# Batch 1's last 256 tokens in 64-token chunks, its first state products and batch 0's half-row states as narrower matmul tiles

## The chip, the cores and the metric

The kernel runs on one core of a Trainium2 chip. The metric is the device time of one execution in microseconds (us). A core has TensorE for matmuls (PE in the profile, with PEld for its weight loads), VectorE (DVE), ScalarE (ACT), GpSimd (POOL), and SyncE (SP), which here issues the DMAs. Each engine works through its own queue of instructions in order and waits for the others by semaphores. Matmul results land in PSUM, eight banks of 128 partitions x 2 KB, from where DVE or ACT copy them to SBUF.

## The reference

Eight batches of 576 tokens, eight heads of 64. First a retention attention without softmax, then a feed-forward layer whose activation is a Silu with its own slope per column:

```
scores = scale * q @ k.T                       # per batch and head, 576 x 576
ret    = scores * gamma_h ** (i - j) for i >= j, else 0
x      = ret @ v                               # heads side by side: 4608 x 512
h      = x @ w_in                              # 512 -> 2048
out    = (h * sigmoid(beta * h)) @ w_out       # 2048 -> 512
```

As the decay is a product, `gamma ** i * gamma ** -j`, it is put into q and v as factors per token (`gq`, `gv`), and the attention can go chunk by chunk: in a chunk, masked scores times v; from all chunks before it, q times a state, which is the running sum of k.T @ v (64 x 64 per head).

## The kernel before

**Tiling.** Batches are worked on in the order 0 to 6, then a block of all batches' last 64 tokens, then 7. The first 512 tokens of a batch are one MLP block, and the eight last pieces of 64 tokens together make the ninth. For a block, `up` makes 128 columns of h for 512 tokens with four matmuls (over 128 rows of w_in each, `KO` = 4) and ACT's Silu writes `gT`; `down` makes 128 tokens of the output with 16 matmuls over `gT` and w_out. `up` can also do half of the tokens (256 columns). Its PSUM tiles come from the tag `mm`, which has three banks; the tags `O` and `sc` have two each, `st` one.

**Attention.** Heads go in four pairs; a pair fills 128 partitions, 64 per head. A state product over 128 tokens as a whole-row matmul computes 128 x 128 for a pair, of which the two 64 x 64 blocks on the diagonal are needed. `d_st`, `d_sc` and `d_out` (batches 2 to 7) work in chunks of 64 tokens with 64 x 64 tiles, four of which lie in different quarters of the PE array: states, scores, and outputs with what earlier chunks add (`cross`). `d_st` returns a `chain` that sums states on DVE into `warm` and `first` in turn and has ACT cast each sum to bf16 (`sbq`, halves of the `sbd` tiles). For heads 4 to 7 these batches hold k and q in another order of heads (`turned`, `head_of`). Batch 1 (`seq` indices 4 to 7) has its own functions with chunks of 128: `pre` and `pre_q` scale and cast, `t_q` and `t_k` transpose on PE, `a_sc` makes scores and masks them on DVE, `a_st` the states, which accumulate in PSUM, `a_O` the chunk's own output, `a_cross` what earlier chunks add with block-diagonal `sbds`, and `a_x` copies to `xT`. Batch 0 has functions `s_*` over two spans of 256 tokens. `s_st(a, n, s, rows)` makes the states of heads 4a to 4a + 3 and of span s over all 128 partitions or the lower or upper half of them; `s_keep` casts them into `sbds`.

**Order.** The schedule is written by hand, engine by engine as the calls come. The head is a straight list of calls (it starts with `warm_up`); in it `keep_warm` is a matmul of 512 columns whose result nobody reads. After it, the list `fill` holds the MLP's steps, and `streams` hold the rest, each with a place in `fill` before which it goes; `merged` weaves them. `d0` is where batch 0's `down` starts and `u1` where batch 1's `up` starts. Batch 1's first ten 128-column pieces of h are made in halves, all first halves and then all second ones, so that the second half of its attention (chunks 6 and 7) can go between them.

Of the kernel before, what the change touches and what calls it, by code (L numbers as in the profile page):

```python
# [11 lines left out]
F32 = mybir.dt.float32  # L12
# [7 lines left out]
def kernel(  # L20
# [46 lines left out]
    NQ = 6  # L67
    E = CB
    XB = 2
    QB = 2  # L70
    HT = MB // 2
    VB = 4
    q_tiles, kv_tiles = {}, {}
# [208 lines left out]
    def pre_q(b, n):  # L282

        if n == 0:
            batch[b] = dict(qs=sb.tile([P, CB, H, D], BF16, name="qs", tag="qs", bufs=2),
                            qT=sb.tile([P, CB, HP, P], BF16, name="qT", tag="qT", bufs=2))
        if b < 2:
            hs, cs = slice(n // 2 * HP, (n // 2 + 1) * HP), slice(n % 2 * 2, n % 2 * 2 + 2)
            e = nc.vector
        else:  # L290
            if n % 2:
                return
            cs = slice(n, n + 2)
            for to, hs in turned:
                nc.gpsimd.tensor_tensor(batch[b]["qs"][:, cs, to], q_tiles[b][:, hs, cs].rearrange("p h i d -> p i h d"),  # L295
                                        gq[:, cs, hs].unsqueeze(3).to_broadcast([P, 2, len(range(H)[hs]), D]), ALU.mult)
            return
        e.tensor_tensor(batch[b]["qs"][:, cs, hs], q_tiles[b][:, hs, cs].rearrange("p h i d -> p i h d"),
                        gq[:, cs, hs].unsqueeze(3).to_broadcast([P, cs.stop - cs.start, hs.stop - hs.start, D]),
                        ALU.mult)  # L300

    def pre(i, js=(0, 1)):

# [57 lines left out]
    def q_cols(i, r, p):  # L361

        b, c = seq[i]
        if b is None:
            return live[i]["qkT"][r, 0, p, :], lambda o: o
        return (batch[b]["qT"][r, :, p, c * PC:(c + 1) * PC], lambda o: o.rearrange("k (i s) -> k i s", i=CB))
# [31 lines left out]
    def a_cross(i):  # L398

        b, c = seq[i]  # L400
        if c == 0:
            return
        for p in range(HP):
            rhs, view = q_cols(i, slice(0, P), p)
            nc.tensor.matmul(view(O_of(i, p)), sbds[c - 1][:, p, :], rhs, start=False, stop=True, skip_group_check=True)

    def a_O(i):

        b, c = seq[i]
        L = live[i]  # L410
        new_O(i)
        R, vn = L["R"], L["vn"]
        for j, p in [(n % 2, n // 2) for n in range(H)]:
            nc.tensor.matmul(O_of(i, p)[j * D:(j + 1) * D], vn[:, 2 * p + j, :], R[:, j, p, :],
                             start=opens(i, p), stop=c == 0, skip_group_check=True)

    def a_x(i):
# [9 lines left out]
    def a_st(i):  # L427

        b, c = seq[i]
        if b is None:  # L430
            return
        L = live[i]
        if c == 0:
            state_ps[b] = psum.tile([P, HP, P], F32, name="st", tag="st", bufs=1)
        st = state_ps[b]
        for p in range(HP):
            nc.tensor.matmul(st[:, p, :], heads(L["kn"], p), heads(L["vn"], p),
                             start=(c == 0 and p == 0), stop=True, skip_group_check=True)
        for j in range(2):
            r, cols = slice(j * D, (j + 1) * D), slice(j * D, (j + 1) * D)  # L440
            e = nc.vector.tensor_copy if i in (CB + 2, CB + 3) else nc.scalar.copy
            if c < CB - 1:
                e(sbds[c][r, :, cols], st[r, :, cols])
                continue
            e(ends[b][r, :2], st[r, :2, cols])
            e(ends[b][(1 - j) * D:(2 - j) * D, 2:], st[r, 2:, cols])

    spread = [(0, 0), (1, 1), (0, 1), (1, 0)]

# [69 lines left out]
    def s_st(a, n, s, rows, at=None, fresh=False):  # L519

        if n not in s_sts:
            s_sts[n] = psum.tile([P, HP, P], F32, name="st", tag="mm" if n else "st", bufs=3 if n else 1)
            fresh = True
        S, at = spans[s], 2 * a if at is None else at
        for i in range(2):
            for p in range(2):
                nc.tensor.matmul(s_sts[n][:, at + p, :], heads(S["kn"][rows, i], 2 * a + p), heads(S["vn"][rows, i], 2 * a + p),  # L527
                                 start=fresh and i == 0 and p == 0, stop=True, skip_group_check=True)
# [25 lines left out]
    def after(later, earlier):  # L554
        tc.add_manual_dep(later.ins, earlier.ins.name, mybir.DependencyInfo(mybir.DependencyClass.Sync, mybir.DependencyReason.DATA))

    def d_sc(u):

        R = [sb.tile([P, 2, 2, HP, TL], BF16, name="R", tag="R", bufs=4) for _ in range(2)]
        sc = {}  # L560
        for x in range(2):
            for j in range(2):
                sc[x, j] = psum.tile([P, 2, HP, TL], F32, name="sc", tag="O" if x else "sc", bufs=2)
            for cl in range(2):
                for p in range(HP):
                    for j, hh in spread:
                        c = 4 * x + 2 * cl + hh
                        nc.tensor.matmul(columns(u, sc[x, j][half(hh), cl, p, :]), piece(u, c)["kT"][half(j), p, half(hh)],  # L568
                                         q_of(u, c, j, p), start=cl == 0 and p == 0, stop=True, skip_group_check=True)
        mask = tri[1 if u == B else 0][:].unsqueeze(1).to_broadcast([P, 2 * HP, TL])  # L570
        batch.setdefault(u, {})["R"] = R

        def masks(x):
            for j in range(2):
                nc.vector.tensor_tensor(R[x][:, j].rearrange("k c p q -> k (c p) q"),  # L575
                                        sc[x, j].rearrange("k c p q -> k (c p) q"), mask, ALU.mult)
        return masks

    def d_st(u, x):

        S = [psum.tile([P, 2, HP, D], F32, name="st", tag=t, bufs=n) for t, n in (("st", 1), ("mm", 3))]
        for cl in range(2):
            for p in range(HP):
                for hh, j in spread:
                    L = piece(u, 4 * x + 2 * cl + hh)
                    nc.tensor.matmul(S[hh][half(j), cl, p, :], L["kn"][half(hh), 2 * p + j, :],  # L586
                                     L["vn"][half(hh), head_of(u, p, j), :], start=cl == 0 and p == 0, stop=True,
                                     skip_group_check=True)

        def chain():  # L590
            for c in range(4 * x, 4 * x + 4):
                new, add = sums[c % 2], S[c % 2][:, c // 2 % 2]
                if c:
                    nc.vector.tensor_tensor(new[:], add, sums[(c - 1) % 2][:], ALU.add)  # L594
                else:
                    nc.vector.tensor_copy(new[:], add)
                nc.scalar.copy((sbq[c] if c < NC - 1 else ends[u])[:], new[:])  # L597
        return chain

    def d_out(u):  # L600
# [42 lines left out]
        return lambda: cross(1), evict  # L643


    gts = {}

    def up(m, fo, c0=0, cn=CB):
# [32 lines left out]
    def down(m, ms, f0, fn=4, n0=0, nn=d_model):  # L681
# [3 lines left out]
            pos_[ms] = psum.tile([P, d_model], F32, name="po", tag="mm" if m or ms < 3 else "st", bufs=3 if m or ms < 3 else 1)  # L685
        po = pos_[ms]
        for fo in range(f0, f0 + fn):
            parts = ((0, nn),) if m or fo < 5 else ((0, nn // 2), (nn // 2, nn))
            for x, y in parts:
                nc.tensor.matmul(po[:, x:y], gT[:, fo, ms, :], w_out_sb[:, fo, n0 + x:n0 + y],  # L690
                                 start=(fo == 0), stop=(fo == FO - 1), skip_group_check=m == 0)
        if f0 + fn < FO:
            return
        if m not in ots:
# [25 lines left out]
    def F(f, *a):  # L720
        return lambda: f(*a)
# [9 lines left out]
    t_q(0, 0)  # L731
    pre_q(0, 2)
    pre_q(0, 3)
    keep_warm()
    t_q(0, 1)
    keep_warm()
    pre_s(0, 0, 0)
    s_T(0, 0)
    pre_s(1, 0, 0)
# [7 lines left out]
    s_sc(1, 0, "mm")  # L747
    pre_s(0, 1, 0)
    pre_s(1, 1, 0)
    keep_warm("st")  # L750
    s_T(1, 1)
    s_sc(0, 1, "sc")
    pre_s(0, 1, 1)
    pre_s(1, 1, 1)
    s_st(0, 1, 0, whole_span)
    s_keep(0, 1, (act, act))
    s_st(0, 0, 0, low)
    s_keep(0, 0, (act, act))
    s_O(0, 0, "O")
    s_sc(1, 1, "mm")  # L760
    s_st(0, 1, 1, low)
# [48 lines left out]
    fill += [F(down_rows, n) for n in range(3)]  # L810
    fill += [F(down, 0, 3, 0)] + [F(down, 0, ms, f0) for f0 in (4, 8) for ms in range(4)] + [F(down, 0, ms, 12) for ms in (3, 0, 1, 2)]

    u1 = len(fill)
    fill += [F(up, 1, fo, 2 * x, 2) for x in range(2) for fo in range(10)]
    fill += [F(up, 1, fo) for fo in range(10, FO)]
    fill += [F(down, 1, ms, f0) for ms in range(MB // P) for f0 in range(0, FO, 4)]
    base = {1: u1 + 10}
    for n, m in enumerate(blocks[2:], 2):
        base[n] = len(fill)
        fill += [F(up, m, fo) for fo in range(FO)]  # L820
# [2 lines left out]
    fill += [F(down, blocks[-1], MB // P - 1, 0, FO, n0, nn) for n0, nn in ((0, 384), (384, 128))]  # L823

    def second(i):
        for f in (a_O, a_cross, a_x):
            f(i)
            f(i + 1)
        a_st(i + 1)

    def triangles():
        nc.gpsimd.memset(causal, 1.0)
# [2 lines left out]
        for t, pattern in zip(tri, ([[1, CB], [CB, TL // CB]], [[1, TL]])):  # L835
            nc.gpsimd.memset(t[:], 1.0)
            for x in range(2):
# [13 lines left out]
               [(d0 + 7, F(pre_q, 1, n)) for n in range(4)] + [(d0 + 12.5, F(pre_q, XB, n)) for n in range(4)] + [(d0 + 11.6, F(t_q, 1, 0)), (d0 + 12.6, F(t_q, 1, 1))],  # L851
               [(d0 + 8, F(pre, 4, (0,))), (d0 + 8, F(pre, 5, (0,))), (d0 + 9, F(pre, 4, (1,))), (d0 + 9, F(pre, 5, (1,))),
                (d0 + 12.7, F(t_k, 4)), (d0 + 14, F(t_k, 5)), (d0 + 14, F(a_sc, 4)), (d0 + 15, F(a_sc, 5)),
                (d0 + 15, F(a_st, 4)), (d0 + 15.9, F(second, 4))],
               [(d0 + 10, F(pre, 6, (0,))), (d0 + 10, F(pre, 7, (0,))), (d0 + 12, F(pre, 6, (1,))), (d0 + 12, F(pre, 7, (1,))),
                (d0 + 15.95, F(t_k, 6)), (u1 + 1, F(t_k, 7)), (u1 + 2, F(a_sc, 6)), (u1 + 3, F(a_sc, 7)),
                (u1 + 4, F(a_st, 6)), (u1 + 7, F(second, 6))]]


    def early_states(u):  # L860
# [85 lines left out]
```

## Time and profile before

| what | us |
|---|---|
| median of three runs | 297.1 (296.67 to 298.74) |
| the profiled execution | 297.28 |
| its span, first to last instruction | 295.5 |
| PE busy | 287.1 |
| ACT busy | 145.9 |
| POOL busy | 111.1 |
| DVE busy | 102.5 |

The profile is one execution. "Busy" is the time in which an engine has at least one instruction under way; matmuls are pipelined, so a matmul's own duration (about 0.2 to 0.4 us) is longer than the time until the next may start, and the time from start to start tells what a matmul costs in a row. The chain of work that ended last follows from the last instruction back to what released each step; its pieces in order of time show which engine set the pace where. "L690" is line 690 of the kernel: 690 is `down`, 655 `up`, 670 `ups` (`up` in two steps, for batch 0), 248 `keep_warm`, 352 `t_q`, 358 `t_k`, 474 and 475 `s_T`, 490 `s_sc`, 504 `s_O`, 512 `s_cross`, 527 `s_st`, 378 `a_sc`, 405 `a_cross`, 414 `a_O`, 437 `a_st`, 586 `d_st`, 568 `d_sc`, 614 and 627 `d_out`, 594 and 597 the sums and casts of `chain`.

### The profile page before, as it was taken

What the parts mean: (1) busy time and instruction counts of PE and PEld (TensorE: products, weight loads), DVE (VectorE), ACT (ScalarE), POOL (GpSimd) and SP (SyncE); (2) the same over time, 40 slices, a digit from 0 to 9 for tenths busy, and PEclk for the clock granted to TensorE, in tenths of its full rate; (3) what the DMA queues carried; (4) which work ended last, traced back from release to release, by engine and by line L of the source; (5) the groups of instructions that cost most, each with busy time, mean ns of one, the idle gap of its engine ahead of it and who ended that gap; (6) DMA issues with size and microseconds to landing.
All of it is one profiled execution on the core that took longest, in us unless ns stands there. A gap on an engine that the chain in (4) does not pass through costs nothing.

```text
span 295.5 us, 7656 instructions
## 1 busy us (share of the span) xinstructions
PE 287.1 (97%) x3245; PEld 150.6 (51%) x3274; DVE 102.5 (35%) x213; ACT 145.9 (49%) x255; POOL 111.1 (38%) x219
## 2 busy tenths in 40 slices
PE   7999999999999999999999999999999999999995
PEld 3654587855544554445444544454554544444443
DVE  5764546604640551045204530354053500110012
ACT  5657537783278434843474347434780167007600
POOL 5957027955733713280438316754223000000000
PEclk9999999999999999999999999999999999999999
DMA  7999999999999898949999849998998110131011
GB/s 225 306 367 386 376 226 277 220 180 253 222 229 235 214 162 231 252 72 161 231 250 198 180 105 273 190 177 180 219 174 138 73 38 0 35 71 38 0 71 71
DMA packets 124033, 53.97 MB, mean 183 GB/s; under 512 B 101840, under 2 KB 116448, under 8 KB 124000
## 3 DMA queue, kind: packets, MB, share of 16 engines
q1 hardware_dynamic: 123968, 53.49, 82.1%
q8 instruction: 25, 0.41, 0.6%
q14 instruction: 8, 0.07, 0.1%
q10 hardware_dynamic: 32, 0.01, 0.0%
HBM read 36.71 MB, written 9.44 MB: 156 GB/s over the span
## 4 chain that ended last, share of the span: by engine, by line
PE 96%; DMA 1%; issue 1%; ACT 0%; DVE 0%; DVEq 0%
PE po L690 42%; PE ph L655 38%; PE ph L670 4%; PE O L614 2%; PE sc L568 1%; PE st L586 1%; DMA qn<-in_q_dram 1%; PE O L627 1%; PE T L352 1%; PE st L527 1%; PE sc L378 0%; PE sc L490 0%; PE O L504 0%; ACT kT L475 0%; PE ph L248 0%
## 5 line engine op out<-in xcount | busy, mean ns | idle before, releaser
L690 PE MATMUL po<-w_out_sb,gT 128*128 128x512 bf16 (+3 forms) x619 | 125.7, 358 | 2.3 <-issue 2.1
L657 ACT ACTIVATE gT<-ph,beta_sb 128x512 bf16<-128x512 f32 (+1 forms) x140 | 91.5, 659 | 50.9 <-PE ph L655 50.5
L655 PE MATMUL ph<-xT,w_in_sb 128*128 128x512 bf16 (+1 forms) x550 | 114.4, 364 | 0.5
L690 PEld LDWEIGHTS <-gT 128*128 128x128 bf16 x636 | 60.2, 98 | 60.7
L655 PEld LDWEIGHTS <-w_in_sb 128*128 128x128 bf16 x560 | 54.3, 98 | 57.5 <-DVE first L594 0.4
L697 DVE COPY ot<-po 128x512 f32<-128x512 f32 (+2 forms) x33 | 22.2, 672 | 72.2 <-PE po L690 69.4
L328 POOL CAST kn<-kvn 128x128 bf16<-128x128 f32 (+2 forms) x76 | 23.4, 343 | 46.1 <-DMA kvn<-in_k_dram 41.2
L295 POOL TENSOR_TENSOR qs<-qn,gq 128x256 bf16<-128x256 f32 (+1 forms) x36 | 26.3, 756 | 33.1 <-DMA qn<-in_q_dram 33.1
L575 DVE TENSOR_TENSOR R<-sc,tri 128x512 bf16<-128x512 f32 x28 | 17.4, 684 | 60.0 <-PE sc L568 60.0
L306 POOL TENSOR_TENSOR vn<-kvn,gv 128x512 bf16<-128x512 f32 x28 | 29.1, 1040 | 7.4 <-DMA kvn<-in_v_dram 7.1
L642 ACT CAST xT<-O 128x512 bf16<-128x512 f32 x14 | 7.5, 590 | 31.6 <-PE O L627 31.6
L597 ACT CAST sbd<-warm 128x256 bf16<-128x256 f32 x18 | 7.3, 407 | 25.6 <-DVE warm L594 20.6
L670 PE MATMUL ph<-xT,w_in_sb 128*128 128x512 bf16 x54 | 12.8, 379 | 0.1
L594 DVE TENSOR_TENSOR first<-st,warm 128x256 f32<-128x256 f32 x24 | 10.2, 425 | 2.9 <-ACT sbq L597 0.5
L316 POOL TENSOR_TENSOR kn<-tln,gq 128x128 bf16<-128x128 f32 (+1 forms) x12 | 5.6, 470 | 14.2 <-DMA tln<-in_q_dram 9.9
L594 DVE TENSOR_TENSOR warm<-st,first 128x256 f32<-128x256 f32 x18 | 7.6, 423 | 9.6 <-PE st L586 8.4
L673 ACT ACTIVATE gT<-ph,beta_sb 128x512 bf16<-128x512 f32 x14 | 8.7, 688 | 4.4 <-PE ph L670 4.4
L642 DVE CAST xT<-O 128x512 bf16<-128x512 f32 x14 | 9.0, 686 | 5.1 <-PE O L627 5.1
L214 POOL CAST w_in_sb<-wt 128x256 bf16<-128x256 f32 (+1 forms) x15 | 7.7, 530 | 5.0 <-DMA wt<-in_moe_w_in_dram 4.9
L597 ACT CAST sbd<-first 128x256 bf16<-128x256 f32 x18 | 7.3, 407 | 2.2 <-DVE first L594 0.2
L670 PEld LDWEIGHTS <-w_in_sb 128*128 128x128 bf16 x56 | 5.2, 97 | 6.3 <-issue 0.5
L231 DVE TENSOR_SCALAR w_out_sb<-wt,rbeta_sb 128x512 bf16<-128x512 f32 x13 | 5.9, 485 | 5.0 <-DMA wt<-in_moe_w_out_dram 5.0
(107 smaller groups left out, 166.1 us busy)
## 6 DMA issues: line engine op xcount, KB each, us to landing
qn<-in_q_dram SPq DMA_DIRECT2D x16, 512.0 KB, 5.2
kvn<-in_k_dram SPq DMA_DIRECT2D x32, 256.0 KB, 6.1
kvn<-in_v_dram SPq DMA_DIRECT2D x32, 256.0 KB, 5.1
out_dram<-ot SPq DMA_DIRECT2D x31, 256.0 KB, 3.4
wt<-in_moe_w_out_dram SPq DMA_DIRECT2D x8, 512.0 KB, 8.5
wt<-in_moe_w_in_dram SPq DMA_DIRECT2D x5, 512.0 KB, 8.8
wt<-in_moe_w_in_dram SPq DMA_DIRECT2D x6, 256.0 KB, 5.6
tln<-in_q_dram SPq DMA_DIRECT2D x8, 128.0 KB, 3.6
```

The source lines that it names most:

```text
L295: nc.gpsimd.tensor_tensor(batch[b]["qs"][:, cs, to], q_tiles[b][:, hs, cs].rearrange("p h i d -> p i h d"), gq[:, cs, hs].unsqueeze(3).to_ ...
L306: nc.gpsimd.tensor_tensor(live[i]["vn"], kv_tiles.pop(i)[:, 1], gains(gv, c), ALU.mult)
L328: nc.gpsimd.tensor_copy(kn[:, c % 2, to], t[:, 0, hs])
L575: nc.vector.tensor_tensor(R[x][:, j].rearrange("k c p q -> k (c p) q"), sc[x, j].rearrange("k c p q -> k (c p) q"), mask, ALU.mult)
L594: nc.vector.tensor_tensor(new[:], add, sums[(c - 1) % 2][:], ALU.add)
L597: nc.scalar.copy((sbq[c] if c < NC - 1 else ends[u])[:], new[:])
L642: (nc.scalar.copy if n % 2 else nc.vector.tensor_copy)(x, o)
L655: nc.tensor.matmul(ph, w_in_sb[:, ko, fo * P:(fo + 1) * P], xts[m][:, ko, :, w], start=(ko == 0), stop=(ko == KO - 1))
L657: nc.scalar.activation(gts[m][:, fo, :, w], ph, ACT.Silu, scale=beta_sb[:, fo:fo + 1])
L670: nc.tensor.matmul(phs[f][:], w_in_sb[:, ko, f * P:(f + 1) * P], xts[m][:, ko], start=(ko == 0), stop=(ko == KO - 1))
L690: nc.tensor.matmul(po[:, x:y], gT[:, fo, ms, :], w_out_sb[:, fo, n0 + x:n0 + y], start=(fo == 0), stop=(fo == FO - 1), skip_group_check=m ...
L697: (nc.scalar.copy if m == 0 else nc.vector.tensor_copy)(ot, po[:, :nn])
```

## The change

Batch 1 takes the turned order of heads too (`QB` from 2 to 1; its q and k casts split into more instructions for that). Its first two chunks stay 128 tokens long, but their states are 128 x 64 tiles, one per head, and `a_cross` uses 64 x 64 tiles; `a_keep` copies the state to `sbq` on ACT and, after the second chunk, to `first` on DVE. Its last 256 tokens go in four chunks of 64: `late_scores` (states, sums and scores, with `d_st` and `d_sc`) before the fourth `up` half, and the new `half_out` before the eleventh, in place of `a_sc`, `a_st` and `second` for chunks 6 and 7. `d_st` takes an `O` bank in place of `mm` there, two of the four sums are cast on DVE in place of ACT, and the last sum goes straight to `ends`. Thirteen 128-column pieces of batch 1 are made in halves, not ten. In the head, three `keep_warm` are left out, `s_st` over half rows for heads 0 to 3 uses 64 x 64 tiles, and `s_st(0, 0, 0, low)` with its `s_keep` goes ahead of `s_st(0, 1, 0, whole_span)`. `down` splits a matmul of 512 columns into two of 256 for other pieces than before: in batch 0 from piece 7 on (was 5), in batch 1 from piece 10 on (was none).

```diff
-    QB = 2
+    QB = 1
...
     def a_cross(i):
 
         b, c = seq[i]
-        if c == 0:
-            return
         for p in range(HP):
-            rhs, view = q_cols(i, slice(0, P), p)
-            nc.tensor.matmul(view(O_of(i, p)), sbds[c - 1][:, p, :], rhs, start=False, stop=True, skip_group_check=True)
+            for j in range(2):
+                rhs, view = q_cols(i, half(j), p)
+                nc.tensor.matmul(view(O_of(i, p)[half(head_of(b, p, j) % 2)]), sbq[2 * c - 1][half(j), p, :], rhs,
+                                 start=False, stop=True, skip_group_check=True)
...
         for p in range(HP):
-            nc.tensor.matmul(st[:, p, :], heads(L["kn"], p), heads(L["vn"], p),
-                             start=(c == 0 and p == 0), stop=True, skip_group_check=True)
...
+            for j in range(2):
+                nc.tensor.matmul(state_ps[b][half(j), p, :], L["kn"][:, 2 * p + j, :], L["vn"][:, head_of(b, p, j), :],
+                                 start=c == 0 and p == 0, stop=True, skip_group_check=True)
+
+    def a_keep(i):
+
+        b, c = seq[i]
+        nc.scalar.copy(sbq[2 * c + 1][:], state_ps[b][:])
+        if c:
+            nc.vector.tensor_copy(sums[c % 2][:], state_ps[b][:])
...
         S, at = spans[s], 2 * a if at is None else at
+        if a == 0 and rows != whole_span:
+            for i in range(2):
+                for p in range(2):
+                    for j in range(2):
+                        nc.tensor.matmul(s_sts[n][half(j), at + p, half(j)], S["kn"][rows, i, 2 * p + j, :],
+                                         S["vn"][rows, i, 2 * p + j, :], start=fresh and i == 0 and p == 0, stop=True,
+                                         skip_group_check=True)
+            return
...
-        def chain():
-            for c in range(4 * x, 4 * x + 4):
-                new, add = sums[c % 2], S[c % 2][:, c // 2 % 2]
+        def chain(cs=range(4 * x, 4 * x + 4), e=nc.scalar.copy):
+            for c in cs:
+                new, add = sums[c % 2] if u != 1 or c < NC - 1 else ends[u], S[c % 2][:, c // 2 % 2]
...
-                nc.scalar.copy((sbq[c] if c < NC - 1 else ends[u])[:], new[:])
+                if new is not ends[u]:
+                    e((sbq[c] if c < NC - 1 else ends[u])[:], new[:])
...
+    def half_out(u):
+
+        O = {(hh, y): psum.tile([P, 2, CB, 2, TL // CB], F32, name="O", tag="sc" if y else "O", bufs=2)
+             for y in range(2) for hh in range(2)}
+        seen = set()
+
+        def to(c, p, x):
+            return O[c % 2, p // 2][half(x), p % 2, :, c // 2 % 2]
+
+        for other in range(2):
+            for n in range(16):
+                cl, pp, y, hh = n // 8, n // 4 % 2, n // 2 % 2, n % 2
+                p, j = pp + 2 * y, hh if other else 1 - hh
+                h = head_of(u, p, j)
+                last = nc.tensor.matmul(to(CB + 2 * cl + hh, p, h % 2), piece(u, CB + 2 * cl)["vn"][half(hh), h, :],
+                                        columns(u, batch[u]["R"][1][half(hh), j, cl, p, :]),
+                                        start=(hh, y, h % 2) not in seen, stop=False, skip_group_check=True)
+                seen.add((hh, y, h % 2))
+            if not other:
+                fence = nc.vector.memset(fenced[:], 0.0)
+                after(fence, last)
+        for flip in range(2):
+            for n in range(16):
+                cl, pp, y, j = n // 8, n // 4 % 2, n // 2 % 2, n % 2
+                c, p = CB + 2 * cl + (j ^ flip), pp + 2 * y
+                m = nc.tensor.matmul(to(c, p, j ^ y), sbq[c - 1][half(j), p, :], q_of(u, c, j, p),
+                                     start=False, stop=True, skip_group_check=True)
+                if flip and n < 2:
+                    after(m, fence)
+        for n, ((hh, y), o) in enumerate(O.items()):
+            x = xt(u)[:, 2 * y:2 * y + 2, :, MB // CB // 2:].rearrange("k p i (c h s) -> k (p i) c h s", c=2, h=2)
+            (dve, act)[n % 2](x[:, :, :, hh, :], o.rearrange("k p i c s -> k (p i) c s"))
...
-            parts = ((0, nn),) if m or fo < 5 else ((0, nn // 2), (nn // 2, nn))
+            parts = ((0, nn),) if m > 1 or fo < (10 if m else 7) else ((0, nn // 2), (nn // 2, nn))
...
     pre_q(0, 3)
-    keep_warm()
     t_q(0, 1)
-    keep_warm()
     pre_s(0, 0, 0)
...
     pre_s(1, 1, 0)
-    keep_warm("st")
     s_T(1, 1)
     s_sc(0, 1, "sc")
     pre_s(0, 1, 1)
     pre_s(1, 1, 1)
+    s_st(0, 0, 0, low)
     s_st(0, 1, 0, whole_span)
+    s_keep(0, 0, (act, act))
     s_keep(0, 1, (act, act))
-    s_st(0, 0, 0, low)
-    s_keep(0, 0, (act, act))
     s_O(0, 0, "O")
...
     def second(i):
-        for f in (a_O, a_cross, a_x):
-            f(i)
-            f(i + 1)
+        a_O(i)
+        a_O(i + 1)
         a_st(i + 1)
+        a_cross(i + 1)
+        a_x(i)
+        a_x(i + 1)
+        a_keep(i + 1)
+
+    def late_scores():
+        chain, masks = d_st(1, 1), d_sc(1, (1,))
+        chain((4, 5), dve)
+        chain((6, 7))
+        masks(1)
...
-                (d0 + 15, F(a_st, 4)), (d0 + 15.9, F(second, 4))],
+                (d0 + 15, F(a_st, 4)), (d0 + 15, F(a_keep, 4)), (d0 + 15.9, F(second, 4))],
...
-                (d0 + 15.95, F(t_k, 6)), (u1 + 1, F(t_k, 7)), (u1 + 2, F(a_sc, 6)), (u1 + 3, F(a_sc, 7)),
-                (u1 + 4, F(a_st, 6)), (u1 + 7, F(second, 6))]]
+                (d0 + 15.95, F(t_k, 6)), (d0 + 15.96, F(t_k, 7)), (u1 + 3, late_scores), (u1 + 10, F(half_out, 1))]]
```

## The prediction, made before the changed kernel was run

> **What bounds the kernel now.** I read the page first: busy times, then the chain of work that ended last.
>
> ```profile
> PE 287.1 (97%) x3245; PEld 150.6 (51%) x3274; DVE 102.5 (35%) x213; ACT 145.9 (49%) x255; POOL 111.1 (38%) x219
> PE 96%; DMA 1%; issue 1%; ACT 0%; DVE 0%; DVEq 0%
> ```
>
> TensorE (PE) is busy for 287.1 of 295.5 us and carries 96% of the chain, so the time is PE's order of work plus PE's waits. What leaves PE counts one for one as long as what PE needs next has arrived; work on another engine costs nothing until PE waits for it. The change touches two stages, so I then read the chain piece by piece there. The head (columns: start us, us, what):
>
> ```profile
> 7.03 0.43 PE ph L248
> 8.43 0.43 PE ph L248
> 8.86 0.44 PE T L474 x4
> 9.32 0.59 ACT kT L475
> ...
> 11.80 0.32 PE ph L248
> 12.12 0.22 PE T L474 x4
> 12.35 0.35 PE sc L490 x16
> 12.69 0.66 PE st L527 x8
> ...
> 15.16 1.00 PE st L527 x16
> 16.15 0.57 PE O L504 x32
> ```
>
> Two things are to be seen. Four transposes cost 0.44 us at 8.86 and 0.22 at 12.12: PE runs at half pace until about 10 us (a 512-column filler 0.43 us, later 0.22). And eight state products cost 0.66 us where sixteen cost 1.00: plain spacing is 56 ns, eight are 0.45, and the rest is two changes between half-row and whole-row matmuls, about 0.1 us each.
>
> Batch 1's second half, in the same view, and ScalarE's (ACT) Silus there by the timeline:
>
> ```profile
> 50.11 0.22 PE T L358 x4
> 50.77 0.46 PE sc L378 x8
> 51.77 0.33 PE sc L378 x8
> 54.18 0.57 PE O L414 x16
> 54.74 0.55 PE O L405 x8
> ```
> ```profile
> 55.99 2.22 ACT L657 ACTIVATE gT<-ph,beta_sb 128x256 bf16<-128x256 f32 x5 [1.30 <-PE ph L655]
> ```
>
> A 256-column Silu takes 476 ns, 437 apart; PE makes such a block in four matmuls of 109 ns, 436. ACT just keeps pace and can't catch up, and three `mm` banks are all that PE may run ahead.
>
> **The parts.** The profiled execution took 297.28 us, 1.78 outside its span of 295.5; the median of the runs shown is 297.1 (296.67 to 298.74). I add to 297.28.
>
> *Head: three fillers out, heads 0 to 3's half-row states as 64x64 tiles in another order.* The first filler covers a wait: the transposes of 7.46 stand for eight, of which the last four wait for VectorE's (DVE) fourth `qs`, done at 7.76 in any case. So it gives 0. The second delays the first key transposes from 8.29 (POOL's cast ends at 8.23) to 8.65: 0.36 us sooner. The scores then start at 9.6, still at half pace, so only 0.2 arrives at DVE's eight masks; they run back to back from 11.84 (598 ns each), and end 0.2 sooner, at 15.3. The third filler gives 0.23 to `s_sc(0, 1)`, but the next states need POOL's values (done 12.24), so PE waits from 12.06 to 12.29. Eight tile states after 64x64 scores need no change of mode: about 0.13 us (four pairs at 32 ns, the spacing of L586's quads), against 0.33. But the new order puts `s_keep(0, 0)` ahead of `s_keep(0, 1)` on ACT, four casts of about 0.27 from 12.65 to 13.72, and `s_st(0, 1, 1, low)` writes the bank that the second pair reads: it starts at 13.77 against 13.85 now. From there the tile form gives 0.2 again, ACT's third keep 0.15, and the whole-row states and `s_O` follow as now: the first `ups` at 16.51 against 16.65, **-0.14**. The last half-row states (at 19.86, 0.65 over the blocks) save a change and 0.1: **-0.10**. The weights allow it: pieces 2 to 7 of w_in are cast 1.4 us or more before use.
>
> *Batch 1.* The price of a burst is the time from the last MLP matmul before it to the first after it, less that matmul's own. Starts in the trace give: `d_st` x32 0.70; with `d_sc` x64 behind it 1.28. So 32 more tiles cost 0.29, and a burst 0.41 for entering and leaving. Now the six bursts from 47.90 to 55.35 cost 1.49, 0.22, 0.56, 0.43, 0.22 and 1.34: 4.26. After: (a) `second(4)` with both `t_k`: 0.49 (`a_O`) + 0.13 (states as 128x64; bounds 0.11, quads' spacing, and 0.22, as `a_O`'s pairs; I take the first's side) + 0.22 (cross, diagonal pairs) + 0.22 + 0.22 + 0.3 for changes, and PE waits 0.33 in `t_k(7)`, whose `sc` bank ACT empties at 49.64 (its 0.39 us copy runs behind the 0.59 of `a_x(4)`): 1.91. (b) `late_scores`: 0.41 + 64 x 0.0091 = 0.99. (c) `half_out`: 0.99, and 0.16 for its fence, since the memset came 0.31 us after the last product before and another 0.1 goes by until PE resumes, while 32 tiles cover only 0.26: 1.15. Sum 4.05, **-0.20**. Three more blocks in halves, 873 against 866 ns: +0.02. The 24 pairs of 256 columns in `down(1)` and the eight fewer in `down(0)` cost 2 ns each: +0.03.
>
> *The new wait.* In the changed ACT order the cast `sbq <- warm` of `late_scores` stands behind the third Silu, and seven Silus behind it. It needs DVE's third sum. Durations are from the same chain at batch 2:
>
> ```profile
> 68.20 0.42 DVE L594 TENSOR_TENSOR first<-st,warm 128x256 f32<-128x256 f32 x1
> 68.73 0.42 DVE L594 TENSOR_TENSOR warm<-st,first 128x256 f32<-128x256 f32 x1
> ```
>
> Dependent ops stand 0.53 apart; DVE starts 0.25 after the last state product (call it s). Sum, cast, sum, cast, sum: the third starts at s + 0.25 + 2 x 0.53 + 2 x 0.15 = 1.6 (a cast of 256 columns took 0.22 alone, 0.43 beside POOL: up to 2.0). ACT follows 0.46 later and holds the next Silu until s + 2.45. That Silu must free the bank of the fourth block after the burst: s + 2.97. PE, with 32 score tiles (0.27), the way out (0.35) and three blocks (1.31) behind it, is there at s + 1.93. It stands **+1.05** (to +1.4). ACT's pace lets it regain nothing; but the masks end at s + 3.85, and `half_out` at s + 4.75 doesn't wait for them, which without the stall would cost 0.2.
>
> POOL's kn casts in three pieces (0.98 for 0.61) and DVE's `qs` in six ops hide in waits for DMA (kn of chunk 7 starts 0.6 after the one before ends; `t_k(7)` comes 1.8 after it). SP's queue and its order stay; loads go on as they land.
>
> Sum: -0.24 - 0.20 + 0.05 + 1.05 = +0.66, **297.9 us**. From batch 2 on nothing differs but the shift.
>
> **Rivals.** *The stall isn't there* (ACT runs later or DVE sooner than I set them): -0.24 - 0.20 + 0.05 + 0.2 = 297.1. For it: my chain has five links. Against it: ACT's order is fixed in the program, and only three banks separate it from PE.
>
> *PE's clock opens later: slower.* PE reached full pace at 10.0, after a stretch from 6.6 in which it streamed for some 2.8 of 3.4 us. Without the fillers it streams about 2.3 there, 68%. The stretch before, 3.2 to 6.6, held some 2.5 (72%) and did not open it. If it stays shut until 13.4, twelve transposes, three score groups and the first states run at twice their time; part is hidden by waits for POOL and ACT; the masks end at 15.8 instead of 15.3, `ups` start 0.8 later: 298.7. One stretch more: about 299.9. It decides if the busy share falls below what the clock asks, between 72 and 83% by these two stretches. The granted clock on the page says full throughout and can't settle it; the spacings do. The Trainium skill (TensorE: Matmul & The Clock Gate, Part 1) says that the clock opens after one busy window of about 3.4 us, and that the windows run free of the kernel's start; the row agrees in the pace and in the length of the stretch. By that rule another phase could help either kernel, so the spread of its runs says little; my 10.0 us is one draw.
>
> *The tiles are worth more, or the change does less than it says.* If the head were PE's alone, it would gain all removed PE time after 8.4: 0.43 + 0.23 + 0.2 + 0.2 + 0.1 = 1.2, and without the stall the total is 296.1. Against: POOL's 12.24 and DVE's 15.3 are fixed by their own rows. If states as tiles cost what whole rows did, the head gains 0 and the total is 298.1.
>
> **Numbers.** Forecast (297.9, and the 298.1 next to it) 0.55; no stall 0.18; clock later 0.19; larger gain 0.08. The range reaches from 296.1 (all gain, no stall) to 299.9 (clock two stretches late, or one and a 0.4 longer stall); this leaves out under 2 in 10. Under 1% (3 us, about what a measurement of this kernel can tell from no change) lie nearly all cases: faster by more 0.05, within 0.85, slower by more 0.10, the last from a late clock together with the longer stall.
>
> **What would show it.** ACT idle for some 1.8 us before its `sbq` cast, released by DVE, and a gap on PE of about 1 us at the seventh half block of batch 1; the first `ups` near 16.5; transposes at 54 ns from 10 us on (rival: 107 until 13.4); `half_out` about 1.15 us between MLP matmuls, with no wait for masks. I am wrong if PE shows no gap there, or if a wait for a load appears after 50 us, where chunk 7's values end at 50.2, only 0.5 ahead of `late_scores`.

## The result, and the profile after

| | before | after |
|---|---|---|
| median of 19 runs, us | 297.22 (296.51 to 298.74) | 298.25 (297.07 to 299.26) |
| the profiled execution, us | 297.28 | 297.92 |
| its span, us | 295.5 | 296.2 |

The ratio is 1.0038, with a 95% interval of 1.0027 to 1.0049: slower by about 0.4%. The medians differ by 1.03 us. The forecast was 297.9. One run of those below (301.77, of `e6_before_nofill`) is over 1.5% above the fastest of its kernel and is left out of every median and mean.

The page of the changed kernel, busy times and the chain that ended last:

```profile
PE 288.4 (97%) x3403; PEld 152.4 (51%) x3403; DVE 101.3 (34%) x215; ACT 146.0 (49%) x259; POOL 112.3 (38%) x227
PE 95%; ACT 1%; POOL 1%; DVE 1%; issue 1%; POOLq 0%
```

PE still carries the chain, but ACT, DVE and POOL now own about 1% each, some 3 us apiece. Where they do is in two places. (Lines moved: in the changed kernel `up` is 694, `ups` 709, `down` 729, `d_st` 590, `d_sc` 572, the sums and casts of `chain` 598 and 602, `half_out` 665 and 676, the tile states 525, `s_keep` 540.)

**Batch 1.** The chain piece by piece, start and length in us:

```profile
50.09 1.31 PE ph L694 x12
51.40 0.44 PE st L590 x32
51.84 0.42 DVE warm L598
...
52.29 0.29 DVE sbd L602
52.58 0.34 DVE first L598
...
52.95 0.29 DVE sbd L602
53.24 0.34 DVE warm L598
...
53.60 0.40 ACT sbq L602
54.01 0.38 ACT gT L696
...
54.44 1.91 PE ph L694 x16
56.34 0.38 PE O L665 x32
56.72 0.39 PE O L676 x30
```

Between 51.84 and 54.44 the chain leaves PE: sum, cast, sum, cast, sum on DVE, then ACT's cast, then the Silu that frees a bank, and only then PE goes on. The groups of ACT between 50 and 57 us and PE's row on the page have the two sides of it (busy us, mean ns, idle us before and its releaser):

```profile
L602 ACT CAST sbq<-warm 128x256 bf16<-128x256 f32 x1 | 0.4, 404 | 1.7 <-DVE warm L598 1.7
```
```profile
L694 PE MATMUL ph<-xT,w_in_sb 128*128 128x512 bf16 (+1 forms) x572 | 114.6, 360 | 1.0 <-ACT gT L696 1.0
```

ACT stands 1.7 us for DVE's third sum, and PE 1.0 us for ACT. From start to start, PE's matmuls there are 1.23 us apart, 1.12 more than the plain 0.11.

**The head.** The page's row of the granted clock, in 40 slices, of before and of after:

```profile
PEclk9999999999999999999999999999999999999999
```
```profile
PEclk9799999999999999999999999999999999999999
```

In the second slice, 7.4 to 14.8 us, the clock of the changed kernel was shut for a time. Its record has it open from 5.70, shut from 9.11 to 12.52, then open. Before, it opened at 9.99 and stayed so. (The row shows 9 for the time ahead of the first opening too, where the spacing of the matmuls tells that the pace was half.)

**A walk along both traces.** How much later the same matmul starts in the changed kernel:

| from the start to | later by, us |
|---|---|
| the first `ups` (16.656 before, 16.833 after) | +0.18 |
| `down` at 47.9 | +0.09 |
| batch 1's first `up` half (49.496, 49.925) | +0.43 |
| the last `down` matmul ahead of the burst at 67 us (66.860, 67.278) | +0.42 |
| the burst of outputs at 79 us | +0.47 |
| behind that burst (a matmul without a record counted in, see below) | +0.82 |
| the end of the execution | +0.64 |

Between 49.9 and 67.3 the stall of 1.12 is paid and as much is won back by cheaper bursts; what is left over comes from the head, from `second(4)`, and from a stand of PE near 80 us.

### The profile page after: what moved, and what is told of

It reads as the page before. It is cut to its first block, busy times and chain, and to the rows that moved or that the text cites. A ratio compares the mean times of both kernels' runs of the same rounds, so it can differ in the third digit from the quotient of the medians.

```text
span 296.2 us, 7957 instructions
## 1 busy us (share of the span) xinstructions
PE 288.4 (97%) x3403; PEld 152.4 (51%) x3403; DVE 101.3 (34%) x215; ACT 146.0 (49%) x259; POOL 112.3 (38%) x227
## 4 chain that ended last, share of the span: by engine, by line
PE 95%; ACT 1%; POOL 1%; DVE 1%; issue 1%; POOLq 0%
PE po L729 43%; PE ph L694 38%; PE ph L709 4%; PE st L590 2%; PE O L619 2%; PE sc L572 1%; PE O L632 1%; PE ph L243 1%; PE T L470 1%; PE sc L486 1%; PE st L531 0%; ACT sbd L540 0%; PE T L350 0%; POOL rbeta_sb L259 0%; PE T L356 0%
## 5 line engine op out<-in xcount | busy, mean ns | idle before, releaser
L729 PE MATMUL po<-w_out_sb,gT 128*128 128x512 bf16 (+3 forms) x652 | 128.9, 354 | 0.0
L729 PEld LDWEIGHTS <-gT 128*128 128x128 bf16 x652 | 61.8, 98 | 59.4
L694 PEld LDWEIGHTS <-w_in_sb 128*128 128x128 bf16 x572 | 55.7, 98 | 57.0 <-issue 1.3
L326 POOL CAST kn<-kvn 128x128 bf16<-128x128 f32 (+1 forms) x84 | 24.6, 333 | 45.4 <-DMA kvn<-in_k_dram 45.3
L579 DVE TENSOR_TENSOR R<-sc,tri 128x512 bf16<-128x512 f32 x30 | 18.6, 681 | 59.9 <-PE sc L572 59.9
L598 DVE TENSOR_TENSOR warm<-st,first 128x256 f32<-128x256 f32 x20 | 8.4, 421 | 10.5 <-PE st L590 9.3
L709 PEld LDWEIGHTS <-w_in_sb 128*128 128x128 bf16 x56 | 5.2, 98 | 6.2 <-issue 0.5
```

The source lines that it names most:

```text
L326: nc.gpsimd.tensor_copy(kn[:, c % 2, to], t[:, 0, hs])
L694: nc.tensor.matmul(ph, w_in_sb[:, ko, fo * P:(fo + 1) * P], xts[m][:, ko, :, w], start=(ko == 0), stop=(ko == KO - 1))
L709: nc.tensor.matmul(phs[f][:], w_in_sb[:, ko, f * P:(f + 1) * P], xts[m][:, ko], start=(ko == 0), stop=(ko == KO - 1))
```

## The experiments

Three sets, each timed on one chip beside its own runs of the kernel before: 297.22 (the first four, as for the changed kernel above), 297.42 (the next four), 297.35 (the last two). Each kernel ran 12 times; an interval is 0.4 to 0.6 us to either side, so smaller differences of medians are read only together with lines of the trace.

| kernel | median, us | ratio to before, 95% interval |
|---|---|---|
| `e1_late_cast` | 297.30 | 1.0005 (0.9989 to 1.0021) |
| `e2_fillers` | 297.88 | 1.0026 (1.0010 to 1.0042) |
| `e3_head_only` | 297.61 | 1.0017 (1.0002 to 1.0031) |
| `e4_act_casts` | 297.43 | 1.0012 (0.9996 to 1.0027) |
| `e5_late_fillers` | 296.81 | 0.9988 (0.9973 to 1.0004) |
| `e6_before_nofill` | 297.44 | 1.0017 (0.9996 to 1.0038) |
| `e7_before_states` | 297.56 | 1.0010 (0.9994 to 1.0025) |
| `e8_late_fill_order` | 297.09 | 0.9985 (0.9967 to 1.0002) |
| `e9_spread` | 296.69 | 0.9977 (0.9965 to 0.9990) |
| `e10_spread_tiles` | 296.68 | 0.9982 (0.9969 to 0.9995) |

### Is the stall the cast's place in ACT's queue?

`e1_late_cast` is the changed kernel with ACT's `sbq <- warm` cast three Silus later:

```diff
         chain((4, 5), dve)
-        chain((6, 7))
+        chain((6, 7), lambda *a: waiting.append(a))
         masks(1)
...
+    def sixth():
+        act(*waiting.pop())
...
-                ... (u1 + 3, late_scores), (u1 + 10, F(half_out, 1))]]
+                ... (u1 + 3, late_scores), (u1 + 6, sixth), (u1 + 10, F(half_out, 1))]]
```

> The changed kernel, with ScalarE's cast of the third sum (sbq <- warm) moved behind three more Silus; nothing else. Stall theory: the gap on PE before the seventh half block (1.12 us in the profile of the changed kernel) goes; half_out comes 1.1 earlier and waits about 0.1 to 0.2 for the masks: about 1.0 us less than the changed kernel, 297.2 or level with before. Rival (the loss is the head's or the tiles'): the gap's time comes back at another wait, within 0.2 us of the changed kernel.

297.30, which is 0.95 below the changed kernel. Its chain at the same place:

```profile
50.57 1.31 PE ph L694 x12
51.88 0.38 PE st L590 x32
52.26 0.29 PE sc L572 x32
52.55 3.25 PE ph L694 x28
55.79 0.41 PE O L665 x32
56.21 0.39 PE O L676 x31
```

28 matmuls in a row, with no stand: the same sums and casts are made, but nothing that PE needs is queued behind them. So the stall was the place of one instruction in ACT's queue. (At 55.0 us two of the 28 start 0.085 us further apart than plain spacing; that is all that is left.)

`e4_act_casts` shortens the chain instead, with the first two casts on ACT:

```diff
-        chain((4, 5), dve)
+        chain((4, 5))
```

> The changed kernel with the casts of the fourth and fifth sums on ScalarE too, as in the other batches. Stall theory: VectorE's third sum comes two casts (0.4 us) sooner, so that the gap on PE before the seventh half block shrinks from 1.12 to about 0.75 us, though ScalarE has two casts more; the time is 0.3 to 0.4 less than the changed kernel. Rival (ScalarE's load, not its wait, makes the gap): two more casts of 0.4 us lengthen the gap to 1.5 us or more.

297.43; the stand at the seventh half block is 0.86 us over plain spacing, against 1.12. The DVE casts were in the chain, but taking them out moved the loss more than it removed it. ACT by time:

```profile
51.73 0.41 ACT L602 CAST sbd<-warm 128x256 bf16<-128x256 f32 x1 [0.43 <-DVE warm L598]
52.26 0.41 ACT L602 CAST sbd<-first 128x256 bf16<-128x256 f32 x1
52.74 0.41 ACT L602 CAST sbq<-warm 128x256 bf16<-128x256 f32 x1
53.05 2.94 ACT L696 ACTIVATE gT<-ph,beta_sb 128x256 bf16<-128x256 f32 x7
```

From the end of the Silu before (51.30) to the next one ACT makes none for 1.75 us, three casts and their waits; in the changed kernel it is 2.0 us, one cast and a wait of 1.7. The median fell by 0.82, twice what was expected, while only 0.26 of the stand went. So a difference of medians can't price the stand here: its price is the 1.12 of the trace, and the 0.95 of `e1` agrees with it within the intervals. What else makes `e4` fast is not shown; 5 of its 12 runs have a dip of the granted clock, as told next, against 14 of 19.

### What do the fillers in the head do?

`e2_fillers` is the changed kernel with the three `keep_warm` back in their places; `e6_before_nofill` is the kernel before without them:

```diff
+    keep_warm()
     t_q(0, 1)
+    keep_warm()
     pre_s(0, 0, 0)
...
     pre_s(1, 1, 0)
+    keep_warm("st")
     s_T(1, 1)
```

> The changed kernel with the three fillers back. Stall theory: the gap at the seventh half block stays at 1.1 us; the fillers only cost or hide, the time is within 0.3 us of the changed kernel. Rival (PE's clock): with the fillers the granted clock is full from its opening on in more of the runs, where the changed kernel had it closed again from 9.1 to 12.5 us in its profile, and the time falls by 0.4 to 1.0 us.

> The kernel before without its three fillers, nothing else. Clock theory: the granted clock dips in more than half of the runs (9 of 12 with the whole head changed, 4 of 35 in the kernel before), and the time is 0.3 to 0.6 over the kernel before. Rival (the tile states or their order cost the head's 0.4): the time is level with before or 0.1 to 0.2 under it.

297.88, 0.37 below the changed kernel, though the stand in its profile is 0.19 longer, 1.31 us (a slow cast on DVE, see below). And 297.44 without fillers, level with its own before in the median (+0.02) and 0.4 above it in the mean, since two runs come near 300: dips in 10 of 12 runs, as the clock theory has it, but not its 0.3 to 0.6 in the median. `e3_head_only` puts all of the head's change into the kernel before, `e7_before_states` the tiles and the order but keeps the fillers (the diff is the head's part of the change, in `e7` without the three lines of `keep_warm`):

> The kernel before with the head's part of the change alone: three fillers out, half-row states of heads 0 to 3 as 64x64 tiles, and their new order. By the prediction's sum 0.24 us less than before. Rival (PE's clock): where the clock shuts again between 9 and 12.5 us, the first MLP matmul comes 0.2 us later than in the kernel before in place of 0.14 earlier, and the time is 0 to 0.5 us over it.

> The kernel before with the tile states and their new order in the head, the fillers kept. Clock theory: few dips of the granted clock, and the prediction's gain of the states: 0.1 to 0.2 under the kernel before. Rival (the tile states or their order cost the head's 0.4): 0.2 to 0.4 over it.

+0.39 and +0.14 against their own before. The second fits neither side: few dips (2 of 12), but not the gain of 0.1 to 0.2, nor the rival's loss of 0.2 to 0.4. In the four pairs with and without fillers (`e2` and the changed kernel, `e6` and before, `e7` and `e3`, and `e5` and `e1` below) the fillers are worth 0.37, 0.02, 0.25 and 0.69, each against its own before: 0.33 on average, all but the last within their intervals.

Most of it goes with the granted clock. Of the runs of all kernels without fillers, 43 of 67 have a mean clock below 0.996, a stretch of 3.4 us at half pace or more; with fillers 23 of 165. (In the four profiles that have one, it lies in the head. A first opening that comes late doesn't show in this mean: `e1`'s profile opened at 13.45 and has 1.000.) Within one kernel the runs with such a dip were on average 0.2 to 1.0 us longer (where more than one run had one, and more than one had none), 0.5 over all of them. An estimate from these numbers: 0.5 us in 64% of the runs against 14% makes 0.25 of the 0.33. Busy times in the stretch of 3.41 us that begins when the clock first opens (columns: window, its length, busy us of PE and count, of PEld, DVE, ACT, POOL, clock of the row, share of DMA, GB/s). First the changed kernel, with the stretch that follows:

```profile
5.70:9.11 3.41, 2.03 (x21) 1.01 (x18) 2.25 (x4) 1.56 (x2) 2.82 (x5) 1.00 1.14 293
9.11:12.52 3.41, 3.31 (x57) 2.31 (x61) 1.95 (x4) 1.34 (x4) 3.27 (x4) 0.50 1.17 291
```

Then the two next to the border, `e9_spread` (below; it has the fillers) and `e4_act_casts`:

```profile
4.20:7.62 3.42, 2.15 (x17) 0.97 (x17) 2.62 (x4) 1.90 (x4) 2.03 (x4) 1.00 1.14 322
```
```profile
6.34:9.76 3.42, 2.18 (x37) 1.24 (x35) 1.82 (x4) 1.60 (x2) 3.07 (x5) 1.00 1.17 292
```

In the changed kernel and in `e9` PE was busy for 2.03 and 2.15 us of that stretch, and the next one ran at half clock; so it was in `e6` with 1.71 and in `e2` with 2.12. In `e4` it was busy for 2.18, and the clock stayed open; so it did in `e3` with 2.27 and in the other four profiles whose clock opened before 8 us, with 2.29 to 2.47. So in these ten profiles a clock just opened shut again when PE was busy for less than about 63% of the next stretch. This order was found after the runs. The weight loads (PEld) part the ten as well, up to 1.10 us and from 1.12 on, so which activity counts isn't shown. The Trainium skill (TensorE: Matmul & The Clock Gate, Part 1) has windows of 3413 ns that run free of the kernel's start; the records agree, with stretches of 3.41 us. It has the clock go back after an idle window; here one with PE busy for 59% was enough. The fillers add busy time just there; where the stretch falls early, as in `e2` and `e9` (from 4.5 and 4.2), not enough. When a shut clock opens doesn't follow from the busy time: `e6` ran at half pace from 7.67 to 17.91, through stretches with PE busy for 2.93, 3.41 and 3.42 us. That is open.

With the clock open in time, the head came near the forecast: `e7` starts its first `ups` at 16.45 and `e3` at 16.49, against 16.66 before (forecast 16.51). But that is no clean price of the tiles. The profile of the kernel before opened its clock only at 9.99, and `e5` and `e10` (both below), with one and the same head and an opening at 6.16 and 5.83, start at 16.47 and 16.19. The head's limit is then POOL, by `e7`'s chain:

```profile
10.16 1.00 POOL kn L467
11.16 2.00 POOL vn L467 x2
13.16 0.56 POOL vn L465
```

### Both mended

`e5_late_fillers` is `e1_late_cast` with the fillers, `e8_late_fill_order` that with `s_st(0, 1, 0, whole_span)` and its `s_keep` ahead again:

```diff
-    s_st(0, 0, 0, low)
     s_st(0, 1, 0, whole_span)
-    s_keep(0, 0, (act, act))
+    s_st(0, 0, 0, low)
     s_keep(0, 1, (act, act))
+    s_keep(0, 0, (act, act))
```

> The changed kernel with the late cast and the three fillers back. Theory of two causes (the stall, and the clock that shuts again in most runs without fillers): both gains add, 1.0 for the stall and 0.3 to 0.5 for the fillers: 296.8 to 297.0, 0.2 to 0.4 under the kernel before, and the granted clock dips in no more than 3 of 12 runs. Rival (the fillers are dead weight, and the clock's dips come from chance): as the late cast alone, 297.3.

> As the kernel with late cast and fillers, and the half-row states of the head behind the whole-row ones again, still as tiles, so that ScalarE casts the shared bank first. The gap of 0.5 us on PE ahead of s_st(0, 1, 1, low), where PE waits for ScalarE's second pair of casts, shrinks to under 0.1, and the first MLP matmul comes 0.2 to 0.3 sooner: about 296.6. Rival (what follows waits for VectorE's masks anyway): level with the kernel with late cast and fillers.

296.81 and 297.09, below before by 0.6 and 0.3, both intervals just reaching 1. `e5` came out as expected, with a dip in 1 run of 12. `e8` did not: PE's gap ahead of `s_st(0, 1, 1, low)` shrank from 0.49 to 0.15 us and the first `ups` start at 16.12 against 16.47 in `e5`, but the median is 0.28 above `e5`'s in place of 0.2 below. In their profiles a new wait shows. The waits of PE in `e8`, 45 to 60 us (in all, times, longest):

```profile
PE ph L694 <- ACT gT L696: 0.7, 1, 0.7
PE O L665 <- DVE R L579: 0.2, 1, 0.2
```

PE waits for a Silu again (in `e8` alone), and `half_out` for the masks (in both). DVE and POOL by time, start and length in us, of `e8`:

```profile
51.96 0.95 DVE L602 CAST sbd<-warm 128x256 bf16<-128x256 f32 x1
...
53.28 0.70 DVE L602 CAST sbd<-first 128x256 bf16<-128x256 f32 x1
```
```profile
51.72 1.04 POOL L297 TENSOR_TENSOR qs<-qn,gq 128x512 bf16<-128x512 f32 x1 [1.11 <-DMA qn<-in_q_dram]
53.22 3.39 POOL L297 TENSOR_TENSOR qs<-qn,gq 128x256 bf16<-128x256 f32 x5 [0.45 <-DMA qn<-in_q_dram]
```

The casts took 0.29 us in the changed kernel and in `e1`; here 0.95 and 0.70. The first starts inside a POOL multiply that ends at 52.76, and ends at 52.91, 0.15 behind it. The second begins inside the first of the five multiplies that the next row holds, which ends at 53.83, and ends at 53.98. One of 0.67 in `e5` and one of 0.48 in `e2` also end 0.15 behind the end of the POOL multiply in which they began. The casts of 0.29 began ahead of a multiply, or in its last 0.11 us. The Trainium skill (SBUF — State Buffer, Who interferes with whom) says that a DVE cast can run in a mode in which it shares one pair of ports with GpSimd, that whoever issues first holds the pair for the whole instruction, and that ACT never waits for anyone: the ends agree. Moving the work in time by half a us decides whether the chain meets POOL's multiply.

So the last two kernels have no late cast on DVE. `e9_spread` (from `e8`) has all three on ACT, apart from each other; `e10_spread_tiles` is the same with the changed kernel's order in the head:

```diff
-        chain((4, 5), dve)
-        chain((6, 7))
+        chain((4,))
+        chain((5, 6, 7), lambda *a: waiting.append(a))
         masks(1)
...
+    def cast():
+        act(*waiting.pop(0))
...
-                ... (u1 + 3, late_scores), (u1 + 10, F(half_out, 1))]]
+                ... (u1 + 3, late_scores), (u1 + 5, cast), (u1 + 7, cast), (u1 + 10, F(half_out, 1))]]
```

> The changed kernel with the three fillers back, the whole-row state products ahead of the half-row tiles again, and all of the late sums' casts on ACT, spread: the first right behind the state products, the second before the sixth up half of batch 1 and the third before the eighth. Theory (the casts on DVE are what makes the masks late, since one took 0.67 to 0.95 us beside POOL's multiply against 0.29 alone, and half_out then waits): with the casts off DVE the masks end some 0.6 us earlier than with the late cast and fillers, half_out needs about 0.9 us with no wait for masks, no gap at the seventh half block, the median about 296.4, 0.5 to 0.7 below the two kernels with late cast and fillers. Rival (ACT has no room for 0.8 us of casts, since it only keeps pace with PE's half blocks): a PE gap of 0.3 to 0.5 us that ACT ends between the sixth and the tenth half block, and a median of 297.0.

> As the one before, but with the half-row tiles ahead of the whole-row state products, as in the changed kernel. Theory (the order in the head is worth 0.1 to 0.3 us, since the first ups started at 16.1 with the old order and 16.5 with the new one): 296.6. Rival (that difference is one draw of the clock's phase): equal to the one before within 0.1. In both, the granted clock should dip in at most 2 of 12 runs, as in the other kernels with fillers.

296.69 and 296.68, 0.66 and 0.67 below their before, with intervals that leave out 1: faster than the kernel before by about 0.2%, and so than the changed one. ACT and PE's chain in `e9`:

```profile
52.67 0.41 ACT L602 CAST sbd<-warm 128x256 bf16<-128x256 f32 x1 [0.43 <-DVE warm L598]
52.98 0.90 ACT L696 ACTIVATE gT<-ph,beta_sb 128x256 bf16<-128x256 f32 x2
53.78 0.40 ACT L882 CAST sbd<-first 128x256 bf16<-128x256 f32 x1
54.08 0.84 ACT L696 ACTIVATE gT<-ph,beta_sb 128x256 bf16<-128x256 f32 x2
54.80 0.41 ACT L882 CAST sbq<-warm 128x256 bf16<-128x256 f32 x1
```
```profile
52.40 3.25 PE ph L694 x28
55.64 0.38 PE O L665 x32
56.02 0.40 PE O L676 x30
```

ACT waits only 0.43 us, and PE from 52.4 on not at all; three casts of 0.4 us between Silus fit in the room of three banks. The theory held in the trace, its size didn't: each against its own before, `e9` gained 0.33 on `e8` and 0.05 on `e5`, where 0.5 to 0.7 was expected, and with intervals of 0.4 these numbers are loose. The order in the head made no difference in the medians, as the rival said, nor much in the start of the first `ups`: 16.19 in `e10`, against 16.12 in `e8` with the other order.

## Why the prediction was right, and which of its steps were not

The time came out 0.35 above the forecast, on the same side and inside the range. The likeliest case, the stall, was the one that happened, by the mechanism that was forecast. Two of the other terms were off, and that they cancel is luck: the bursts by −0.60 and the head by about +0.63. (A slip besides: with no gain in the head the terms give 298.2, not 298.1.)

- **The stall**, forecast at +1.05: 1.12 in the trace, and 0.95 in the medians when one cast was moved (`e1`). The chain of five links was right: third sum at s + 1.6, measured 53.16 with the last state product's start, s, at 51.58. ACT stood 1.7 us, forecast 1.8. That DVE's casts beside POOL might stretch it, the "up to 2.0", didn't happen in this profile but did in `e8`, where the third sum came at s + 2.65.
- **The bursts**, forecast at −0.20: −0.80. From the last MLP matmul to the next, less its own, they took 1.83 (forecast 1.91), 0.76 (0.99) and 0.87 (1.15), 3.46 in all against 4.26 before. The step that failed is the price of a burst, 0.41 for entering and leaving. Why shows in two rows of each page, `down`'s matmuls and their weight loads, first before, then after:

```profile
L690 PE MATMUL po<-w_out_sb,gT 128*128 128x512 bf16 (+3 forms) x619 | 125.7, 358 | 2.3 <-issue 2.1
...
L690 PEld LDWEIGHTS <-gT 128*128 128x128 bf16 x636 | 60.2, 98 | 60.7
```
```profile
L729 PE MATMUL po<-w_out_sb,gT 128*128 128x512 bf16 (+3 forms) x652 | 128.9, 354 | 0.0
...
L729 PEld LDWEIGHTS <-gT 128*128 128x128 bf16 x652 | 61.8, 98 | 59.4
```

  Every matmul has a weight load. Before, 619 matmuls stand against 636 loads: 17 have no record, and the `issue` that the row has, 2.1 us, stands in 13 pieces of about 0.16, each right behind a burst. The forecast took the next recorded matmul for the first. After, with 652 and 652, the `issue` is gone. With the missing 0.23 us put back, `d_st` cost 0.47, not 0.70, and with `d_sc` 1.05, not 1.28: 0.18 for entering and leaving. So late_scores and half_out were each priced 0.23 too high. The rest is 0.08 in `second(4)` with the `t_k` and 0.05 in `half_out`, whose fence was priced at 0.16.
- **The head**, forecast at −0.24: −0.29 in a profile whose clock opened once (`e7`: 0.21 by the first `ups`, 0.08 more by the first `down`, beside a profile of the kernel before whose clock opened 5 us later), but +0.39 in `e3`'s median, +0.14 in `e7`'s and +0.09 in the changed kernel's trace at 47.9 us. So what the tiles alone are worth in the head stays open. What failed is the filler's part: the second filler's price of 0.36 was read from what follows it on PE; that it can also keep the clock open was weighed only as a delayed opening, not as one that is taken back. The changed kernel's first `ups` came at 16.83: its transposes at 9.85 and 11.81 took 0.54 us for four, half pace, where 54 ns each from 10 us on had been named as the sign. PE's wait of 0.3 us for ACT's casts of `s_keep`, which the forecast of 13.77 contained, came at 14.11.
- **The rival with the clock** was near in its prices: with an opening at 13.45 (`e1`) the first `ups` start 0.66 later than before, forecast 0.8 for 13.4; with one at 17.91 (`e6`) 2.55 later, where the forecast has 2.0 for two stretches (299.9 against 297.9). The length of a stretch, with which it set 6.6 and 13.4, stands in no row of the kernel before; four later records have it, 3.41 us. It was wrong on when: "between 72 and 83%" is not what decided. The busy share told the outcome once the clock was open, with a border at 63%; a shut clock opened after a stretch with 3.07 us of busy time in `e5` and with 3.14 in `e3`, and not after 3.12 in `e1`.
- **The masks** were no wait, as forecast for the case with the stall: they end at 55.23, and `half_out` starts at 56.27. Without the stall they cost next to nothing in `e1` and the forecast 0.2 us in `e5`, where a cast was held up. `t_k(7)` waited for ACT's copy, 0.2 us where 0.33 was forecast. PE waited for no load.

With the terms as measured, −0.80 and 1.12 and the head's +0.39 from `e3`, the sum is +0.71; the medians differ by 1.03. 0.3 of that is in no term, which is within the interval of `e3` alone. One candidate is a stand near 80 us. In the changed kernel the chain has there:

```profile
80.25 0.07 PE O L632 x3
80.33 0.19 issue
80.52 0.38 PE O L632 x24
```

and in `e7_before_states`:

```profile
78.86 0.54 PE O L622 x48
79.40 0.72 issue
80.11 0.31 PE O L622 x13
```

PE stops within a burst and waits for nothing that the profile shows. Less a missing record where there is one, that burst took 1.54 us in six of the profiles, 1.65 to 1.68 in four (before is one), 2.01 in the changed kernel's and 2.42 in `e7`'s. So it makes 0.36 of the 0.64 between the two profiled executions, and is enough to make `e7`'s (297.52) no faster than before although its head is. What it is, and whether it comes more often in one kernel than in another, stays open.

## What to carry to other kernels

An engine that waits in order for a chain elsewhere holds up everything queued behind it: put such an instruction as late in the queue as its reader allows. Here one cast three places later took away a stand of 1.12 us on PE, and the median fell by 0.95; only with the stand gone and the fillers back did the smaller tiles show a gain. A matmul that nobody reads is not free to delete in a stretch where PE is otherwise idle, since its busy time can keep the clock open. And before a price is taken from the distance of two records, count the records: matmuls against weight loads.

## What the runs showed of the hardware that was not expected

- A clock that has just opened can shut again after one stretch of 3.41 us in which PE is far from idle: by ten profiles it did with up to 2.15 us of busy time and didn't from 2.18 on, a border at about 63%. Whether PE's matmuls or its weight loads count is open.
- A DVE cast from SBUF to SBUF that begins within a POOL multiply ends 0.15 us after it: 0.48, 0.67, 0.70 and 0.95 us for 0.29. One that began in the last 0.11 us of a multiply lost nothing that shows.
- A burst of 64 x 64 tiles between 128 x 128 matmuls costs 0.18 us for entering and leaving, beside 9 ns a tile: 0.47 for 32 tiles, 0.76 for 64, 1.05 for 96.
